# Rotated token inputs formed 1024 columns at a time, attention masks added behind the scores, constants loaded first, and a new table of leads

## Chip, core and metric

The program runs on one core of a Trainium2 chip. The time is the device time of one execution in microseconds (us); lower is better. Inputs lie in the chip's memory in a layout that the host prepares once and that is not timed.

## What is computed

The reference chains three blocks over 2 batches of 768 tokens, everything in float32:

```python
# 1. attention, 8 heads of 64: a window of 31 keys around each query, and the maximum of each block of 32 keys
scores_l = where(|s - t| < 16, scale * q @ k.T, -1e9)
scores_s = scale * q @ max_over_blocks(k) + log(32)
a = softmax(concat(scores_l, scores_s));  x = a @ concat(v, mean_over_blocks(v))
# 2. token mixing by rotation
theta = x @ w_theta
y = w_tok_r @ (x * cos(theta)) + w_tok_i @ (x * sin(theta))
u = x + y;  x2 = u + relu(u @ w_ch)
# 3. gated unit
h = gelu(x2 @ w_in);  u, v = halves(h)
v_s = w_sg @ (layernorm(v) * g) + b_sg
out = x2 + (u * v_s) @ w_out
```

## The kernel before

The eight (batch, two heads) pairs of the attention are worked one after another, each in two halves of 384 queries. For one half, TensorE (PE) forms the scores `S` of two heads, VectorE (DVE) takes the row maxima `nb` (L723), ScalarE (ACT) the exponentials `P` (L728), PE turns `P` round (`PT`, L737), ACT or DVE copies it out (`Pt`), PE multiplies with the values (`O`, L756), DVE divides (`x`, L783), and PE turns the result (`X`, L795) into `xT`. Before that, keys and sums of keys are laid into windows (`kv<-k`, `kv<-ks`) and sums of values (`vsp`, L659) are spread into the value tiles (`kv<-vs`), by whichever of ACT, DVE and GpSimd (POOL) the planner picks.

The 32 score tiles begin with a mask: `masks` multiplies a table of 0 and -8e9 by a bf16 identity with `start=True`, and `mm` adds the products of queries and keys to it (L702, L712).

Every float32 product behind the attention is done as three matmuls of split operands (`mm3`, L443 to L445): high times high, high times low, low times high. `hi_of` makes the high part (ACT, DVE or POOL, L431 to L438), `lo_of` subtracts it for the low part (DVE or POOL, L461). Weights come as raw bits and are put together by a rebias (L552 on ACT, L554 on POOL), three steps on DVE (L541 to L547), and a high and a low part.

The input of the token mixing is split into `xs` (one per 128 tokens, 12 in all), multiplied by `w_th` to angles `th`, reduced to within pi (`rr`), and turned by `rotated(n)`: `abs`, `cos` and `sin` on ACT, then for each of cosine (`cc`) and sine (`rr`) a product with `x` (L876), a high and a low part (`zs`), each over 512 columns. `y_big` and `y_small` multiply them with `w_r`, `w_i` and `w_ri`. From there on (`u`, `ch`, `v`, `sg`, `o`) nothing is edited.

The order of the work is not written out. All operations are declared with a cost per engine, a planner (`Plan`) gives each a due time from the order in which PE work is declared, less a lead by kind (`BIAS`), and plays them out: each engine takes the ready operation that is due first, an operation with a choice of engines goes where cost times a load factor (`LOAD`) is least, and buffers come from pools of a fixed count (`HOMES`). What comes out is one fixed order per engine. SyncE (SP) issues the loads in the order of `PLAN["want"]`; a load that finds no free buffer holds all loads behind it. Each load also waits for the one eight places before it to land.

Where the played-out PE has a gap of over 0.25 us before the operation `warm_end`, filler matmuls are put in (`fill`, L1128, result `wps`, unused); twelve more on zeros open the program (`warm`).

Of the kernel before, what the change touches and what calls it, by code (L numbers as in the profile page):

```python
# [49 lines left out]
class Plan:  # L50
# [266 lines left out]
    "M": 25, "PT": -2, "S": -1, "abs": 4, "ba_": -5, "blocks": 25, "bs_": 8, "bsg": -24,  # L317
    "ch___": -2, "cos": 19, "craw": -6, "g": -5, "gf__": -8, "gm__": -5, "gs__h": -1,
    "gs__l": 15, "id": -18, "ident": 4, "k": 1, "ki": 7, "kk": 13, "kw_": -19, "mask": -10,
    "max": 1, "norm_": 1, "o___": -7, "ob__": 12, "q": -14, "q_": -2, "quarter": -9, "ra": 4,  # L320
    "rb": -4, "rc": -11, "rec_": -3, "sg___": -14, "sin": -6, "small": -4, "sq": 2,
    "st__": 26, "th_": -9, "uT__": 13, "u___": -7, "us__h": 2, "us__l": 8, "v_": -17,
    "v__": 7, "vf_": -4, "vnh_": -4, "vnl_": 21, "vs_": 16, "vsc": -7, "vsg": 1, "vsp": 2,
    "w_ch.": 1, "w_ch.h": -9, "w_ch.hi": -7, "w_ch.lo": 13, "w_i.": -3, "w_i.h": 8,
    "w_i.hi": -12, "w_i.lo": 7, "w_inu.": -9, "w_inu.h": 10, "w_inu.hi": 4, "w_inu.lo": 13,
    "w_inv.": -4, "w_inv.h": 1, "w_inv.hi": 4, "w_inv.lo": -10, "w_out.": 6, "w_out.h": 11,
    "w_out.hi": -14, "w_out.lo": -2, "w_r.": -18, "w_r.hi": -1, "w_r.lo": 9, "w_ri.": 5,
    "w_ri.h": -1, "w_ri.hi": 1, "w_ri.lo": -6, "w_sg.": 8, "w_sg.hi": 24, "w_sg.lo": -7,
# [7 lines left out]
LOAD = ({"ACT": 0.71, "DVE": 1.34, "POOL": 0.92}, {"ACT": 0.08, "DVE": 1.79, "POOL": 23.66},  # L336
        80.0)
# [17 lines left out]
def kernel(  # L355
# [497 lines left out]
    def rotated(n):  # L853

        b, i = divmod(n, NT)
        rr, cc = f"rr{n}", buf(f"cc{n}", "t")
        hf, t = divmod(i, 3)
        x = f"x{b}_{hf}"

        def away(e):  # L860
            if e is ACT:
                e.activation(T(cc)[:], T(rr)[:], AF.Abs)
            else:
                e.tensor_scalar(out=T(cc)[:], in0=T(rr)[:], scalar1=0.0, scalar2=None,
                                op0=ALU.abs_max)
# [2 lines left out]
        op(f"cos{n}", {"ACT": 0.73}, lambda e: ACT.activation(
            T(cc)[:], T(cc)[:], AF.Sin, bias=half_pi[:], scale=-1.0), [cc, "consts"], [cc],
           table="trig", after=last_exp)  # L870
        op(f"sin{n}", {"ACT": 0.62}, lambda e: ACT.activation(T(rr)[:], T(rr)[:], AF.Sin),
           [rr], [rr], table="trig", after=last_exp)
        for k, z in enumerate((cc, rr)):
            zs = f"zs{n}_{k}"
            pair(zs)
            op(f"z{n}_{k}", {"DVE": 0.69, "POOL": 1.28}, lambda e, z=z: e.tensor_tensor(  # L876
                out=T(z)[:], in0=T(z)[:], in1=T(x)[:, t * DM:(t + 1) * DM], op=ALU.mult),
               [z, *((x, r) for r in range(NP))], [z], port=True)
# [4 lines left out]

    def y_big(n):

        b, i = divmod(n, NT)
        for d in range(4):
# [3 lines left out]
            for k, key in enumerate(("r", "i")):  # L891
                op(f"y{n}_{d}_{k}", {"PE": 0.685}, lambda e, d=d, k=k, key=key, y=y: mm3(
                    T(y)[:], cut(hl_of(f"zs{n}_{k}"), sl(d)), unit((key, i)),
                    i == 0 and k == 0, i == NT - 1 and k == 1),
                   [*both(f"zs{n}_{k}"), *has((key, i))], [y])

    def y_small(n):

        b, i = divmod(n, NT)
        for d in range(4):  # L900
# [4 lines left out]
            def mm(e, d=d, y=y):  # L905
                for k in range(2):
                    mm3(T(y)[:, sl(d % 2, 256)], cut(hl_of(f"zs{n}_{k}"), sl(d)),
# [451 lines left out]
```

## Time and profile before

| | us |
|---|---|
| median of 3 runs | 403.67 |
| lowest and highest run | 397.71, 406.56 |
| the profiled execution, device time | 399.96 |
| its span, first to last instruction | 398.2 |
| PE busy within the span | 388.1 |
| DVE, ACT, POOL busy | 282.5, 199.6, 49.0 |

The profile records one execution. A row of `lines` gives a source line, the engine, what is written from what, shape and count, then busy time and mean ns of one instruction, then the idle time before it. A matmul's duration holds its way through the array, so back to back ones overlap: a step from one to the next is shorter than the mean. A row of `windows` gives the busy time of each engine within a stretch, the number of instructions, the granted PE clock, the share of time in which the DMA engines were busy (somewhat over 1 where records overlap) and GB/s. In `waits`, a row says who waited for whom, for how long in total, how often, and the longest.

### The profile page before, as it was taken

The page shows a single profiled execution, that of the slowest core. Times are in us where ns is not written, and L with a number is a line of the kernel's source. Part 1 is how long each engine was busy: PE and PEld are TensorE (multiplying, and loading weights), DVE is VectorE, ACT ScalarE, POOL GpSimd, SP SyncE. Part 2 cuts the span into 40 slices and gives each one's busy share as a digit, 9 for nine tenths or more (in the row PEclk, how much of TensorE's full clock was granted, in tenths as well). Part 3 has the DMA queues.
Part 4 walks back from the last instruction along what each step waited for, and adds up shares of the span by engine and source line. Part 5 has one row for each costly group of instructions (what it writes and reads, how often), then busy time and mean ns, then how long its engine had stood idle before and what let it go on. Part 6 is the DMA issues. An engine that isn't in the chain of part 4 may idle for free.

```text
span 398.2 us, 7273 instructions
## 1 busy us (share of the span) xinstructions
PE 388.1 (97%) x2899; PEld 324.9 (82%) x2899; DVE 282.5 (71%) x542; ACT 199.6 (50%) x415; POOL 49.0 (12%) x81
## 2 busy tenths in 40 slices
PE   7898999999999999999999999999999999999996
PEld 3666667778888888889999988889888889888986
DVE  3769979999999997689999889483454146315442
ACT  3686878668999943244673516274110035411100
POOL 1567886220000000000000000000000000000000
PEclk9999999999999999999999999999999999999999
DMA  8999995310010011338930032010001101000012
GB/s 229 291 282 297 287 252 200 109 54 2 0 34 20 0 54 53 93 96 299 404 130 0 2 106 105 2 53 2 0 0 43 38 28 40 15 0 0 16 44 102
DMA packets 15970, 37.63 MB, mean 95 GB/s; under 512 B 1984, under 2 KB 4928, under 8 KB 15936
## 3 DMA queue, kind: packets, MB, share of 16 engines
q1 hardware_dynamic: 15936, 37.16, 30.0%
q8 instruction: 23, 0.38, 0.4%
q14 instruction: 11, 0.09, 0.1%
HBM read 34.01 MB, written 3.15 MB: 93 GB/s over the span
## 4 chain that ended last, share of the span: by engine, by line
PE 86%; DMA 9%; DVE 3%; SPq 1%; ACT 1%; issue 0%; DVEq 0%
PE y L444 8%; PE y L443 8%; PE y L445 8%; DMA k<-in_kT_dram 4%; PE sg L445 4%; PE sg L444 4%; PE sg L443 4%; PE th L443 3%; PE ch L445 3%; PE ch L443 3%; PE o L445 3%; PE ch L444 3%; PE o L444 3%; PE o L443 3%; PE u L445 3%; PE u L444 3%
## 5 line engine op out<-in xcount | busy, mean ns | idle before, releaser
L431 ACT ACTIVATE g<-gf 128x512 fp32r<-128x512 f32 (+1 forms) x16 | 8.4, 525 | 59.7 <-DVE gf L1100 59.7
L1097 DVE SCALAR_TENSOR_TENSOR gf<-sg,g_sb,bsg 128x512 f32<-128x512 f32 (+1 forms) x16 | 9.9, 617 | 36.4 <-PE sg L445 36.4
L728 ACT ACTIVATE P<-S,nb 128x120 f32<-128x120 f32 x96 | 27.5, 370 | 8.5 <-DVE nb L723 8.1
L444 PE MATMUL y<-w_ri,zs 128*128 128x256 f32 x96 | 27.1, 282 | 0.0
L443 PE MATMUL y<-w_ri,zs 128*128 128x256 f32 x96 | 27.1, 282 | 0.0
L445 PE MATMUL y<-w_ri,zs 128*128 128x256 f32 x96 | 27.0, 282 | 0.0
L443 PE MATMUL ch<-u,w_ch 128*128 128x512 f32 (+1 forms) x64 | 21.7, 338 | 0.0
L445 PE MATMUL ch<-u,w_ch 128*128 128x512 f32 (+1 forms) x64 | 21.6, 338 | 0.0
L444 PE MATMUL o<-g,w_out 128*128 128x512 f32 (+1 forms) x64 | 21.6, 337 | 0.0
L445 PE MATMUL o<-g,w_out 128*128 128x512 f32 (+1 forms) x64 | 21.6, 337 | 0.0
L444 PE MATMUL ch<-u,w_ch 128*128 128x512 f32 (+1 forms) x64 | 21.6, 337 | 0.0
L443 PE MATMUL o<-g,w_out 128*128 128x512 f32 (+1 forms) x64 | 21.6, 337 | 0.0
L444 PE MATMUL u<-x,w_inu 128*128 128x512 f32 (+1 forms) x64 | 21.5, 336 | 0.0
L443 PE MATMUL u<-x,w_inu 128*128 128x512 f32 (+1 forms) x64 | 21.5, 336 | 0.0
L445 PE MATMUL u<-x,w_inu 128*128 128x512 f32 (+1 forms) x64 | 21.5, 336 | 0.0
L443 PE MATMUL th<-w_th,xs 128*128 128x512 f32 x48 | 20.3, 424 | 0.0
L445 PE MATMUL sg<-w_sg,vn 128*128 128x512 f32 x48 | 19.0, 397 | 0.0
L444 PE MATMUL sg<-w_sg,vn 128*128 128x512 f32 x48 | 19.0, 395 | 0.0
L443 PE MATMUL sg<-w_sg,vn 128*128 128x512 f32 x48 | 18.9, 393 | 0.0
L444 PE MATMUL y<-w_i,zs 128*128 128x512 f32 x48 | 18.8, 392 | 0.0
L445 PE MATMUL th<-w_th,xs 128*128 128x512 f32 x48 | 18.8, 392 | 0.0
L444 PE MATMUL y<-w_r,zs 128*128 128x512 f32 x48 | 18.8, 392 | 0.0
(197 smaller groups left out, 1167.3 us busy)
## 6 DMA issues: line engine op xcount, KB each, us to landing
k<-in_kT_dram SPq DMA_DIRECT2D x8, 384.0 KB, 8.1
w_r<-in_w_rT_dram SPq DMA_DIRECT2D x6, 512.0 KB, 6.4
w_i<-in_w_iT_dram SPq DMA_DIRECT2D x6, 512.0 KB, 4.6
kv<-in_vW_dram SPq DMA_DIRECT2D x8, 341.2 KB, 9.3
kv<-in_qT_dram SPq DMA_DIRECT2D x7, 384.0 KB, 9.5
w_th<-in_w_theta_dram SPq DMA_DIRECT2D x4, 512.0 KB, 7.9
w_ch<-in_w_ch_dram SPq DMA_DIRECT2D x4, 512.0 KB, 4.7
w_inv<-in_w_in_dram SPq DMA_DIRECT2D x4, 512.0 KB, 6.2
```

The lines of the kernel that those rows point to most:

```text
L431: e.activation(dst, src, AF.Copy, scale=scale)
L443: PE.matmul(ps, ah, bh, start=first, stop=False, skip_group_check=True)
L444: PE.matmul(ps, ah, bl, start=False, stop=False, skip_group_check=True)
L445: PE.matmul(ps, al, bh, start=False, stop=last, skip_group_check=True)
L728: ACT.activation(T(pt)[:, t * WC:(t + 1) * WC], T(ps)[:, t * WC:(t + 1) * WC], AF.Exp, bias=T(nb)[:, t:t + 1], scale=1.0),
L1097: lambda e: DVE.scalar_tensor_tensor(out=T(gf)[:, :n], in0=T(ps)[:, :n], scalar=g_sb[:, f:f + 1], in1=T("bsg")[:, o:o + n], op0=ALU.mult, ...
```

## The change

`rotated` writes cosine and sine side by side into one tile `zz` of 1024 columns: one product with `x` (read twice, by a repeated axis), one high and one low part, instead of two of each; the halves are cut out in `turned_of`. `scores` sets the matmuls of queries and keys first and the masks behind them, and the masks cover only the 96 window columns of each 120 (288 instead of 360). The constants (`craw`: identity and masks) are the second load instead of the third, and a load of one number out of `craw` (`gate`) stands behind the first queries, so that SP goes on to the values only when `craw` has landed. The opening filler is nine matmuls instead of twelve. All leads, load factors, the place of the third and fourth part of `w_th` among the loads, and of `r 1` and `i 1`, are set anew. Of the tables one line each:

```diff
-HOMES = {"w": 31, "t": 7, "c": 3, ...
+HOMES = {"w": 31, "t": 8, "c": 2, ...
-LOAD = ({"ACT": 0.71, "DVE": 1.34, "POOL": 0.92}, {"ACT": 0.08, "DVE": 1.79, "POOL": 23.66}, 80.0)
+LOAD = ({"ACT": 0.85, "DVE": 0.68, "POOL": 1.1}, {"ACT": 0.05, "DVE": 2.51, "POOL": 23.66}, 70.0)
-    "theta": [20, 26, 27, 28, 29, 36],
+    "theta": [20, 21, 26, 29, 31, 32],
...
         else:
-            load("q0_0", lambda: T("kv0_0")[:, :S // 2], qT[b, r][:, :S // 2], [("q", p, 0)])
             buf("craw", "t")
             load("craw", lambda: T("craw")[:, :P + 3 * WC], consts, ["craw"])
-            load("q0_1", lambda: T("kv0_0")[:, S // 2:S], qT[b, r][:, S // 2:], [("q", p, 1)])
+            for x in range(2):
+                c0 = x * S // 2
+                load(f"q0_{x}", lambda c0=c0: T("kv0_0")[:, c0:c0 + S // 2],
+                     qT[b, r][:, c0:c0 + S // 2], [("q", p, x)])
+
+            op("gate", {"SP": 0.06}, lambda e: e.dma_start(gate[:], T("craw")[0:1, 0:1]),
+               ["craw"], ["gate"], dma=0.01)
...
-        def masks(e):
-            for g in gs:
-                PE.matmul(T(f"S{g}")[:, :3 * WC], id16[:], mask[:, hf * WC:(hf + 3) * WC], start=True,
-                          stop=False, skip_group_check=True)
...
-                                  start=False, stop=True, skip_group_check=True)
+                                  start=t == 0, stop=False, skip_group_check=True)
+
+        def masks(e):
+            def keys(x):
+                return x.rearrange("p (t c) -> p t c", c=WC)[:, :, :WK]
+
+            for g in gs:
+                PE.matmul(keys(T(f"S{g}")[:, :3 * WC]), id16[:],
+                          keys(mask[:, hf * WC:(hf + 3) * WC]), start=False, stop=True,
+                          skip_group_check=True)
...
-        for k, z in enumerate((cc, rr)):
-            zs = f"zs{n}_{k}"
-            pair(zs)
-            op(f"z{n}_{k}", {"DVE": 0.69, "POOL": 1.28}, lambda e, z=z: e.tensor_tensor(
-                out=T(z)[:], in0=T(z)[:], in1=T(x)[:, t * DM:(t + 1) * DM], op=ALU.mult),
-               [z, *((x, r) for r in range(NP))], [z], port=True)
...
+        def turn(e):
+            z = T(zz)[:].rearrange("p (k d) -> p k d", k=2)
+            e.tensor_tensor(out=z, in0=z, in1=T(x)[:, t * DM:(t + 1) * DM].unsqueeze(1)
+                            .to_broadcast([P, 2, DM]), op=ALU.mult)
+
+        op(f"z{n}", {"DVE": 1.22, "POOL": 2.4}, turn,
+           [(zz, 0), (zz, 1), *((x, r) for r in range(NP))], [zz], port=True)
...
+        hi_of(f"zh{n}", hi, lambda: T(zz)[:], [zz], [f"zs{n}_h"], 1024)
+        lo_of(f"zl{n}", lo, lambda: T(zz)[:], hi, [zz, f"zs{n}_h"], [f"zs{n}_l"], 1024)
...
-    op("warm", {"PE": 4.5}, lambda e: fill(12, T("zeros")[:].bitcast(BF16)), ["zeros"], ["wps"])
+    op("warm", {"PE": 3.6}, lambda e: fill(9, T("zeros")[:].bitcast(BF16)), ["zeros"], ["wps"])
```

The order on SP at the start of the program, before (`k0` and `kv0_0<-in_qT` are keys and queries of the first pair, `vW` its values, the name ahead of the arrow is the tile that is written):

```order
L472 DMA k0_79<-in_kT_dram 128x768
L472 DMA kv0_0_81<-in_qT_dram 128x384
L472 DMA craw_83<-in_consts_dram 128x488
L472 DMA kv0_0_81<-in_qT_dram 128x384
L472 DMA kv0_2_86<-in_vW_dram 96x520
L472 DMA kv0_3_90<-in_vW_dram 96x910
L472 DMA kv0_0_81<-in_vW_dram 96x130
L472 DMA k1_93<-in_kT_dram 128x768
```

and now:

```order
L472 DMA k0_80<-in_kT_dram 128x768
L472 DMA craw_82<-in_consts_dram 128x488
L472 DMA kv0_0_84<-in_qT_dram 128x384 x2
L501 DMA gate_72<-craw_82 1x1
L472 DMA kv0_2_104<-in_vW_dram 96x520
L472 DMA kv0_3_110<-in_vW_dram 96x910
L472 DMA kv0_0_84<-in_vW_dram 96x130
L472 DMA k1_114<-in_kT_dram 128x768
```

`craw` moved ahead of the first queries, and the values and all later loads stand behind a load that waits for `craw`.

On PE the program opened with twelve fillers, four masks and then the scores of the first pair; S0 to S3 are its four score tiles, `id16` the bf16 identity:

```order
L1128 MATMUL wps_102<-zeros_88 128x480
L702 LDWEIGHTS id16_67
L702 MATMUL S0_173<-mask_68,id16_67 128x360
...
L702 MATMUL S3_179<-mask_68,id16_67 128x360
L712 MATMUL S0_173<-kv0_1_156,kv0_0_81 64x120
L712 MATMUL S1_175<-kv0_1_156,kv0_0_81 64x120
...
L659 MATMUL vsp0_207<-kv0_2_86,blocks_69 24x130 x2
```

and now it opens with:

```order
L1147 MATMUL wps_89<-zeros_87 128x480
L713 MATMUL S0_133<-kv0_1_101,kv0_0_84 64x120
L713 MATMUL S1_135<-kv0_1_101,kv0_0_84 64x120
...
L722 LDWEIGHTS id16_67
L722 MATMUL S0_133<-mask_68,id16_67 128x3x96
...
L722 MATMUL S3_180<-mask_68,id16_67 128x3x96
L1147 LDWEIGHTS id16_67
L1147 MATMUL wps_89<-mask_68,id16_67 128x480
...
L664 MATMUL vsp0_218<-kv0_2_104,blocks_69 24x130 x2
```

The scores come first, the masks and four new fillers stand between them and the sums of values. In all there are 18 fillers on the mask instead of 9, and 9 on zeros instead of 12.

On POOL, where the first angles are prepared (`xs0<-xT` with one source is the high part of 128 tokens' input, with two sources its low part; `w_r` and `w_i` with one source are rebiases, which need the weight's load), it stood before:

```order
L554 TENSOR_SCALAR w_i0_374<-w_i0_374 128x512
L433 TENSOR_SCALAR xs0_887<-xT_75 128x512
L433 TENSOR_SCALAR kv4_2_141<-vs_71 24x520
L461 TENSOR_TENSOR xs0_887<-xT_75,xs0_887 128x512
L461 TENSOR_TENSOR w_th2_928<-cw_th2_815,w_th2_928 128x512
L433 TENSOR_SCALAR xs1_971<-xT_75 128x512
```

and now:

```order
L461 TENSOR_TENSOR w_th2_936<-cw_th2_739,w_th2_936 128x512
L433 TENSOR_SCALAR xs1_1026<-xT_76 128x512
L433 TENSOR_SCALAR xs2_1041<-xT_76 128x512
L559 TENSOR_SCALAR w_r1_731<-w_r1_731 128x512
L559 TENSOR_SCALAR w_i1_737<-w_i1_737 128x512
L461 TENSOR_TENSOR xs1_1026<-xT_76,xs1_1026 128x512
L461 TENSOR_TENSOR xs2_1041<-xT_76,xs2_1041 128x512
```

The rebiases of `w_r1` and `w_i1`, which ACT did before (L552), now stand on POOL between the high and the low part of `xs1`. PE's first angles are now those of `xs1` (before: `xs0`), and ahead of them PE has the whole fifth pair, counted from zero, instead of its first half.

## Rows read from the trace of the kernel before

**Rows 1.** Busy time of each engine in stretches (us from the span's start)

```profile
14.70:53.40 38.70, 34.47 (x607) 25.24 (x607) 31.22 (x69) 29.56 (x85) 27.41 (x45) 1.00 1.05 286
...
60.00:100.00 40.00, 40.00 (x464) 31.32 (x457) 37.88 (x78) 30.79 (x72) 10.84 (x13) 1.00 0.27 89
...
340.00:380.00 40.00, 40.00 (x222) 34.63 (x221) 13.90 (x23) 7.77 (x15) 0.00 (x0) 1.00 0.03 11
```

**Rows 2.** Who waited for whom: PE's waits

```profile
PE X L795 <- DVE x L783: 3.8, 5, 0.9
```

**Rows 3.** PE in order of time, the opening: start us, us, what, count

```profile
1.49 4.98 PE L1128 MATMUL wps<-zeros 128*128 128x480 bf16 x12 [1.49 <-DVE zeros L1137]
7.19 0.77 PE L702 MATMUL S<-mask,id 128*128 128x360 bf16 x4 [0.72 <-DVE mask L438]
7.89 1.46 PE L712 MATMUL S<-kv,kv 64*64 64x120 f32 x48
9.28 2.96 PE L659 MATMUL vsp<-kv,blocks 96*24 96x130 f32 x24
```

**Rows 4.** Groups of PE instructions by line

```profile
L702 PE MATMUL S<-mask,id 128*128 128x360 bf16 x32 | 7.4, 318 | 0.7 <-DVE mask L438 0.7
...
L1128 PE MATMUL wps<-mask,id 128*128 128x480 bf16 x9 | 3.0, 370 | 0.0
```

**Rows 5.** SP in order of time, the first loads

```profile
0.74 0.38 SPq L472 DMA_DIRECT2D k<-in_kT_dram  x1
...
1.64 0.42 SPq L472 DMA_DIRECT2D craw<-in_consts_dram  x1
...
2.58 1.37 SPq L472 DMA_DIRECT2D kv<-in_vW_dram  x3
```

**Rows 6.** Everything on the tile craw: us from issue to landing

```profile
DMA to landing us min/median/max: 4.9/4.9/4.9
```

**Rows 7.** DVE in order of time: the first work on landed keys, the first maxima

```profile
3.71 0.95 DVE L614 TENSOR_REDUCE ks<-k 128x24 f32<-128x768 f32 x1 [2.27 <-DMA k<-in_kT_dram]
...
8.79 1.85 DVE L723 TENSOR_REDUCE nb<-S 128x3 f32<-128x360 f32 x4 [0.96 <-PE S L712]
```

**Rows 8.** Groups of DVE instructions by form

```profile
L876 DVE TENSOR_TENSOR cc<-cc,x 128x512 f32<-128x512 f32 x12 | 8.2, 686 | 0.0
L1100 DVE TENSOR_TENSOR gf<-gf,uT 128x512 f32<-128x512 f32 x8 | 5.5, 692 | 0.3
L1100 DVE TENSOR_TENSOR gf<-gf,uT 128x256 f32<-128x256 f32 x8 | 3.4, 425 | 0.3
L438 DVE COPY Pt<-PT 120x384 f32<-120x384 f32 x3 | 1.6, 549 | 0.2 <-PE PT L737 0.2
L438 DVE COPY kv<-vs 24x910 f32<-24x910 f32 x2 | 2.2, 1094 | 0.1
```

**Rows 9.** PE in order of time: scores of two halves running, the first angles

```profile
46.96 0.85 PE L712 MATMUL S<-kv,kv 64*64 64x120 f32 x24
...
51.13 1.06 PE L712 MATMUL S<-kv,kv 64*64 64x120 f32 x24
...
53.87 0.48 PE L443 MATMUL th<-w_th,xs 128*128 128x512 f32 x1
```

**Rows 10.** SP in order of time, around the first angles

```profile
50.11 1.38 SPq L472 DMA_DIRECT2D w_r<-in_w_rT_dram  x2
57.82 0.33 SPq L472 DMA_DIRECT2D w_i<-in_w_iT_dram  x1
```

**Rows 11.** DMA issues from 46 to 56 us: count, KB each, median us to landing

```profile
w_i<-in_w_iT_dram SPq DMA_DIRECT2D x1, 512.0 KB, 8.6
```

**Rows 12.** POOL, DVE and PE in order of time, first angles and first y

```profile
58.86 1.28 POOL L461 TENSOR_TENSOR xs<-xT,xs 128x512 fp32r<-128x512 f32 x1
...
99.09 0.68 DVE L461 TENSOR_TENSOR zs<-cc,zs 128x512 fp32r<-128x512 f32 x1
...
101.88 0.39 PE L443 MATMUL y<-w_r,zs 128*128 128x512 f32 x1
```

More of the change, by code (lines that the diff above doesn't have):

```diff
@@ L316 @@
 BIAS = {
[L317 to L328, printed above, removed]
@@ L329 @@
-    "w_sgs.": 1, "w_sgs.hi": -8, "w_sgs.lo": 8, "w_th.": 1, "w_th.h": -4, "w_th.lo": -2,
-    "warm": -21, "warm_end": -10, "xT_": -5, "x__": 8, "xh": 2, "xs__h": 3, "xs__l": -13,
-    "y__": 2, "ys_": -14, "z_": 2, "zeros": -13, "zh_": -6, "zl_": -2,
+    "M": 25, "S": -1, "abs": 4, "ba_": -5, "blocks": 25, "bs_": 16, "bsg": -24, "ch___": -6,
+    "cos": 18, "craw": -6, "g": -9, "gf__": -12, "gm__": -5, "gs__h": -6, "id": -22,
+    "ident": 8, "k": 5, "ki": 7, "kk": 13, "ksum": 1, "kw_": -19, "mask": -12, "max": 1,
@@ new lines @@
+    "norm_": 2, "o___": -3, "ob__": 12, "q": -4, "q_": -2, "quarter": -13, "rb": -8, "rc": -9,
+    "rec_": -3, "sg___": -14, "sin": -6, "small": -6, "sq": 2, "th_": -9, "uT__": 13,
+    "u__": -6, "u___": -7, "us__h": -6, "us__l": 8, "v_": -13, "v__": 3, "vf_": -8,
+    "vnh_": -4, "vnl_": 21, "vs_": 14, "vsc": -7, "vsg": 1, "vsp": -6, "vsw_": 4, "w_ch.": 1,
+    "w_ch.h": -9, "w_ch.hi": -7, "w_ch.lo": 13, "w_i.": -3, "w_i.h": 9, "w_i.hi": -12,
+    "w_i.lo": 7, "w_inu.": -17, "w_inu.h": 10, "w_inu.hi": -4, "w_inu.lo": 5, "w_inv.": -2,
@@ new lines @@
+    "w_inv.h": 1, "w_inv.hi": 4, "w_inv.lo": -10, "w_out.": 6, "w_out.h": 11, "w_out.hi": -14,
+    "w_out.lo": 2, "w_r.": -14, "w_r.hi": -1, "w_r.lo": 9, "w_ri.": 4, "w_ri.h": -1,
+    "w_ri.hi": 1, "w_ri.lo": -7, "w_sg.": 8, "w_sg.hi": 24, "w_sg.lo": -7, "w_sgs.": 1,
+    "w_sgs.hi": -7, "w_sgs.lo": 8, "w_th.": 1, "w_th.h": -3, "w_th.lo": -2, "warm": -21,
+    "warm_end": -14, "xT_": -5, "x__": 9, "xh": -2, "xs__h": 7, "xs__l": -13, "y__": 2,
+    "ys_": -14, "z_": 2, "zeros": -13, "zh": 2, "zh_": -6, "zl_": -2,
@@ L334 @@
 STAY = 15.5
-LOAD = ({"ACT": 0.71, "DVE": 1.34, "POOL": 0.92}, {"ACT": 0.08, "DVE": 1.79, "POOL": 23.66},
-        80.0)
+LOAD = ({"ACT": 0.85, "DVE": 0.68, "POOL": 1.1}, {"ACT": 0.05, "DVE": 2.51, "POOL": 23.66},
+        70.0)
 PLAN = {
-    "want": [("pair", 0), ("pair", 1), ("th", 0), ("pair", 2), ("pair", 3), ("th", 1), ("pair", 4),
-             ("th", 3), ("th", 2), ("pair", 5), ("r", 0), ("i", 0), ("pair", 7), ("pair", 6),
-             ("i", 1), ("r", 1)],
+    "want": [("pair", 0), ("pair", 1), ("th", 0), ("pair", 2), ("pair", 3), ("th", 1), ("pair", 4), ("th", 2), ("pair", 5), ("th", 3), ("r", 0), ("i", 0), ("pair", 7), ("pair", 6),
+             ("r", 1), ("i", 1)],
     "ahead": 0,
-    "theta": [20, 26, 27, 28, 29, 36],
+    "theta": [20, 21, 26, 29, 31, 32],
     "filler": 20,
@@ L417 @@
     vs_sb = cp.tile([P, VC], F32, tag="vs", name="vs")
+    gate = cp.tile([1, 1], F32, tag="gate", name="gate")
     half_pi = cp.tile([P, 1], F32, tag="hpi", name="half_pi")
@@ L855, in rotated @@
         b, i = divmod(n, NT)
-        rr, cc = f"rr{n}", buf(f"cc{n}", "t")
+        rr, zz = f"rr{n}", buf(f"zz{n}", "w")
         hf, t = divmod(i, 3)
         x = f"x{b}_{hf}"
+        for k in range(2):
+            plan.at((zz, k), zz)
         def away(e):
             if e is ACT:
-                e.activation(T(cc)[:], T(rr)[:], AF.Abs)
+                e.activation(T(zz)[:, 512:], T(rr)[:], AF.Abs)
             else:
-                e.tensor_scalar(out=T(cc)[:], in0=T(rr)[:], scalar1=0.0, scalar2=None,
+                e.tensor_scalar(out=T(zz)[:, 512:], in0=T(rr)[:], scalar1=0.0, scalar2=None,
@@ L865, in away @@
                                 op0=ALU.abs_max)
-        op(f"abs{n}", {"ACT": 0.62}, away, [rr], [cc], port=True)
+        op(f"abs{n}", {"ACT": 0.62}, away, [rr], [(zz, 1)], port=True)
         op(f"cos{n}", {"ACT": 0.73}, lambda e: ACT.activation(
[L869 to L872, printed above, removed]
@@ new lines, in rotated @@
+           [(zz, 1), "consts"], [(zz, 1)], table="trig", after=last_exp)
+        op(f"sin{n}", {"ACT": 0.62}, lambda e: ACT.activation(T(zz)[:, :512], T(rr)[:], AF.Sin),
+           [rr], [(zz, 0)], table="trig", after=last_exp)
+        def turn(e):
[4 more added lines that the diff above has]
+           [(zz, 0), (zz, 1), *((x, r) for r in range(NP))], [zz], port=True)
@@ L892, in y_big @@
                 op(f"y{n}_{d}_{k}", {"PE": 0.685}, lambda e, d=d, k=k, key=key, y=y: mm3(
[L893 removed]
+                    T(y)[:], cut(turned_of(n, k), sl(d)), unit((key, i)),
                     i == 0 and k == 0, i == NT - 1 and k == 1),
[L895 removed]
+                   [f"zs{n}_h", f"zs{n}_l", *has((key, i))], [y])
     def y_small(n):
@@ L911, in y_small @@
             op(f"ys{n}_{d}", {"PE": 0.73}, mm,
-               both(f"zs{n}_0") + both(f"zs{n}_1") + has(("ri", i)), [y])
+               [f"zs{n}_h", f"zs{n}_l", *has(("ri", i))], [y])
     def x_keys(b, half, d):
```

16 lines of the change are left out of this document (9 added, 7 removed).

## The prediction

> **What bounds the kernel now.** I read the windows first. From 60 us PE is busy without a gap: of eight stretches of 40 us up to 380 us each shows 40.00 us of PE, the first and the last stand in [rows 1]. DVE, ACT and POOL have time left in them. So work taken off DVE, ACT or POOL behind 60 us is worth nothing, and the end can move only through PE's own work, and through gaps ahead of 60 us. In the attention, from 14.7 to 53.4 us, no engine is full [rows 1]: of 38.7 us PE has 34.47, DVE 31.22, ACT 29.56 and POOL 27.41, and only the DMA share (1.05, at 286 GB/s) is at its limit. The waits name one steady wait of PE there: `X` waits for `x` on DVE, 3.8 us in five waits [rows 2]. In order of time the opening comes next [rows 3]: twelve fillers, masks, scores, then `vsp`, which ends at 12.24 us because it waits for the values.
>
> **The sum's base.** Durations come from one execution of 399.96 us, its span 398.2 and 1.76 around it. That is 3.7 below the median of three runs (403.67), inside their 397.71 to 406.56. I sum against 399.96. A measurement of this kernel can tell about 2%, 8.1 us, from no change.
>
> **The change part by part.**
>
> Narrow masks. Each of 32 masks loses 72 of its 360 columns. The price of a column comes from two groups [rows 4]: 480 columns take 370 ns, 360 take 318, so 52 ns for 120 columns, 31 ns for 72; 32 of them give 1.0. PE has gaps around them, so some of it may be hidden; and the read now jumps from block to block, which no row shows. Bounded by a full gain and by the 52 ns as a loss each (32 x 0.052): -1.0 to +1.7. I take -1.0, since the number of columns is what the rows price.
>
> Scores ahead of masks. The first scores stand behind the masks, which wait for a DVE copy of `craw` and start at 7.19 [rows 3]; `craw` is issued at 1.64 [rows 5] and lands 4.9 us later [rows 6]. Now the scores need only keys and queries, `craw` is issued one load (0.4 to 0.5 us) earlier and should land at about 5.2, and the masks end at about 8.2, where the first row maxima could start on scores at 8.79 [rows 7]. Gain 0.6. Bounds: -1.5 if `craw` lands so early that the masks never wait, +0.5 if it lands at 6.5 as before and the masks' 0.77 us then stand behind the scores. I take -0.6.
>
> The gate. SP issues the values at 2.58 [rows 5]; now SP waits for `craw` and goes on at about 5.3. `k` (384 KB), `craw` (244) and `q` (384) are 1.01 MB ahead of it, at 286 GB/s [rows 1] 3.5 us, done at about 6.0 with the start. `k`, issued at 0.74, lands at 3.71 [rows 5, 7], 2.97 us, of which 384 KB at 286 GB/s are 1.35; so 1.6 us of a load is no transfer, and the values' first bytes come at about 7.0. That is a hole of 1.0 us in a stream that is full from the first loads on through the attention [rows 1]. Queued behind the gate on SP is every later load. I take +0.9; bounds 0 (the stream has the slack) and +2.7 (5.3 less 2.58, all of it passed on).
>
> For the part of a load that is no transfer the Trainium skill ("DMA: Bandwidth & Descriptors", section "Anatomy of one DMA — SWDGE (gpsimd) path") states about 2 us, most of it the confirmation that the last byte has landed. By it the hole would be 1.4 us and the term +1.3; the trace's 1.6 us is used. The rule speaks against this edit: a load that waits for another's landing pays that time once more.
>
> Fillers. Three fewer on zeros are 3 x 0.415 [rows 3] off a stretch that ends before the scores can start: worth nothing, covered by the wait for `k` and `q`. Nine more on the mask cost by the price of a column above 480 x 0.43 ns = 0.21 us each, 1.9 in all. Four stand ahead of `vsp`, which waited for values until 12 us in any case; the planner puts the others where it sees gaps. I take +0.5; bounds 0 and +1.9.
>
> Where the helpers of the attention run. By the order, up to the maxima of the twentieth score tile DVE gets seven more copies of `PT` (7 x 0.549 = 3.8 by [rows 8]) and two wide copies of sums of values (2 x 1.094 = 2.2, [rows 8]), 6.0 us, and smaller pieces leave it, on an engine that has 7.5 us free of 38.7 [rows 1], while ACT and POOL get lighter. Against that `X` now stands further behind `O` on PE, so that its waits of 3.8 us [rows 2] could go. What is late next, if they go, is DVE itself with its maxima. I take +0.5; bounds -3.8 (all waits go) and +6.0 (all of DVE's added work reaches the end); the value near nothing, since both ends draw on the same free 7.5 us.
>
> First angles. Ahead of the first `th` at 53.87 PE now has half a pair more, 4.2 us from one half's scores to the next (46.96, 51.13) [rows 9], and six new fillers beside the four counted, 1.3; so it gets there at about 59.4. There it needs the low part of `xs1`, which POOL now does behind the rebiases of `w_r1` and `w_i1`. Two such loads were issued at 50.11, the second ends its issue at 51.49 [rows 10], and one takes 8.6 us to land [rows 11], so between 58.5 and 60.1; I take the early end, since the order wants them sooner. A rebias (an estimate: half of the low part's, with one source for two, 0.64) and the low part (1.28, [rows 12]) give 60.5: PE waits 1.1, with a share of the gate's shift 1.4. Queued behind that `xs1` on POOL is the low part of `xs2`, and on PE the angles of both. Bounds: 0 (the weights land by 57.5) and +8.9 (below).
>
> The rotation. Two products of 686 ns [rows 8] become one of 1024 columns. From 256 to 512 columns a like product goes from 425 to 692 ns [rows 8], 267 for 256; so 692 + 534 = 1.23 us against 1.37, for 24 products and low parts -3.5 us on DVE, and less on ACT too. All of it lies beside a full PE [rows 1]: worth nothing. If the cover is gone, it is at the first `y`: it needs a cosine's low part alone, done at 99.77, 2.1 us ahead of `y` at 101.88 [rows 12]; now it waits for both halves, which costs from 0 to +1.2. I take 0.
>
> Sum: -1.0 - 0.6 + 0.9 + 0.5 + 0.5 + 1.4 + 0 = +1.7, so 399.96 + 1.7 = 401.7.
>
> **The rivals.**
>
> Late weights under POOL (slower). Place: the rebias of `w_i1` ahead of the low part of `xs1`. SP issued two `w_r` at 50.11, but a `w_i` only at 57.82 [rows 10], when a buffer came free. If the first `w_i` needed gets such a late place, it lands at 57.82 + 8.6 = 66.4 [rows 11], the low part ends at 68.3, and PE stands for 8.9 us; at 59.5 the wait is 2.1. The mean is 5.5 in place of 1.4: 405.8. It decides as soon as `w_i1` lands behind 57.5. For it: the queue's rows, and no other work of PE between. Against: the planner sees loads and buffers and placed POOL's row there; PE may also be later than 59.4.
>
> Waits of the attention gone (faster). The 3.8 us of `X` [rows 2] vanish since `X` has more work ahead of it, and the weights land in time: 399.96 - 1.0 - 0.6 + 0.9 + 0.5 - 3.8 = 396.0. For it: the new order sets just these apart, and ACT (29.56 of 38.7) and POOL lose work. Against: DVE, which ends the wait, gets more.
>
> The clock of the opening (slower by a little). The twelve fillers step at 415 ns for 480 columns [rows 3], 1.16 columns to the ns, the level of 1.2 GHz; the four masks behind them go 1440 columns in 0.77 us, above it. With nine fillers PE has been busy for 1.25 us less when the scores start. If these run at the lower level, their 1.46 and the masks' 0.65 double: +2.1, 403.8. Against: the fillers end before the scores in either case and could be enough.
>
> The Trainium skill ("TensorE: Matmul & The Clock Gate", section "Part 1: The HAM clock gate") has the low clock as the resting state, which activity releases; the fillers' step and the masks' agree with it.
>
> That the change doesn't do what it says holds for the rotation: it does save DVE's time, but PE doesn't wait for it.
>
> **How the numbers follow.** Forecast 401.7 (with its own spread of 3 either side) .50; late weights .18; attention waits gone .24; clock .06; something else .02. The range that holds 8 in 10 reaches from the faster rival (396.0, less 1 for the sizes of its terms) to the slower one with its larger waits (399.96 + 0.3 + 8.9 = 409.2): 395 to 409; the forecast's own is 398.7 to 404.7. Faster by over 2% is below 395.6 (of the median): nearly half of the faster rival and a little of the forecast, .16. Slower by over 2% is above 411.7: the late weights at their worst with the gate's 2.7 or the attention's 6.0 on top, .10. The rest, .74, is within 2%.
>
> **What would show it.** In the profile after: first scores at about 6 us, ahead of `craw`'s landing at about 5.2 plus a copy; masks of a mean near 288 ns; a DMA share well under 0.9 in a stretch between 5 and 8 us (the hole); one wait of PE `th` for POOL `xs`, 1 to 2 us long; products of 1024 columns on DVE at about 1.23 us; PE 40.00 of 40 from 60 on. Wrong would make it: a wait of `th` over 4 us (the weights), `X` without waits and DVE not full (the faster rival), first scores of twice 1.46 us (the clock), or a gap of PE behind 60 us that before didn't have, at the first `y` above all.

## The result, and the profile after

The changed kernel takes 405.48 us (median of 20 runs, 401.32 to 407.85), the kernel before 402.73 (20 runs): ratio 1.0111, 95% interval 1.0084 to 1.0137, some 4.5 us slower (1.11% of 402.73). The ratios in this document leave out runs over 1.5% above the fastest of the same kernel, here 7 of 20 before and 2 of 20 after; over all runs the medians differ by 2.75 us, and the means give ratios lower by 0.1 to 0.7 points for every kernel but `e12`. The profiled execution took 403.10 us, its span is 401.3.

The opening first. SP's loads and PE in order of time, changed kernel:

```profile
1.18 0.42 SPq L472 DMA_DIRECT2D craw<-in_consts_dram  x1
...
4.51 0.71 SPq L501 DMA_DIRECT2D gate<-craw  x1
5.27 1.29 SPq L472 DMA_DIRECT2D kv<-in_vW_dram  x3
```

```profile
1.50 3.78 PE L1147 MATMUL wps<-zeros 128*128 128x480 bf16 x9 [1.50 <-DVE zeros L1156]
5.21 2.48 PE L713 MATMUL S<-kv,kv 64*64 64x120 f32 x48
7.62 0.66 PE L722 MATMUL S<-mask,id 128*128 128x288 bf16 x4
8.12 0.97 PE L1147 MATMUL wps<-mask,id 128*128 128x480 bf16 x4
9.02 2.84 PE L664 MATMUL vsp<-kv,blocks 96*24 96x130 f32 x24
```

Against [rows 3, 5]: the values are issued at 5.27 instead of 2.58, the scores start at 5.21 instead of 7.89, but take 2.48 us instead of 1.46. Windows of the changed kernel (columns as in [rows 1]: the last two are DMA share and GB/s):

```profile
4.00:5.00 1.00, 1.00 (x4) 0.17 (x2) 1.00 (x3) 1.00 (x4) 0.69 (x3) 1.00 0.92 343
5.00:6.00 1.00, 1.00 (x17) 0.80 (x20) 0.89 (x6) 0.30 (x2) 0.47 (x2) 1.00 0.01 5
6.00:7.00 1.00, 1.00 (x28) 1.00 (x24) 0.04 (x1) 0.00 (x0) 0.00 (x0) 1.00 0.67 149
...
14.70:53.40 38.70, 33.49 (x596) 24.10 (x592) 31.24 (x70) 25.83 (x82) 18.31 (x35) 1.00 1.04 292
60.00:100.00 40.00, 40.00 (x473) 31.77 (x472) 36.89 (x74) 34.10 (x84) 6.76 (x7) 1.00 0.21 68
```

The stream stands still from 5 to 6 us (5 GB/s) and is half empty to 7. Behind 60 us PE is full as before; the loss lies ahead of it. PE's waits:

```profile
PE X L805 <- DVE ri L796: 3.1, 1, 3.1
PE O L766 <- POOL kv L433: 2.0, 1, 2.0
...
PE O L766 <- DVE Pt L438: 1.0, 2, 0.7
...
PE X L805 <- DVE x L793: 0.3, 1, 0.3
```

The five waits of [rows 2], 3.8 us, are down to one of 0.3; two new ones, 5.1 us, have come. Where they lie, PE and then DVE in order of time:

```profile
46.52 0.97 PE L1147 MATMUL wps<-mask,id 128*128 128x480 bf16 x4
49.46 0.94 PE L766 MATMUL O<-kv,Pt 120*64 120x65 f32 x24 [1.97 <-POOL kv L433]
50.33 0.85 PE L713 MATMUL S<-kv,kv 64*64 64x120 f32 x24
51.11 0.42 PE L722 MATMUL S<-mask,id 128*128 128x288 bf16 x2
51.37 0.37 PE L1147 MATMUL wps<-mask,id 128*128 128x480 bf16 x1
54.82 0.59 PE L805 MATMUL X<-ident,x 128*128 128x128 f32 x3 [3.09 <-DVE ri L796]
55.21 0.85 PE L747 MATMUL PT<-ident,P 128*120 128x128 f32 x3
55.99 1.53 PE L664 MATMUL vsp<-kv,blocks 96*32 96x130 f32 x24
...
61.55 0.48 PE L443 MATMUL th<-w_th,xs 128*128 128x512 f32 x1
```

```profile
48.96 0.54 DVE L438 COPY kv<-vs 24x130 f32<-24x130 f32 x1
51.92 0.95 DVE L619 TENSOR_REDUCE ks<-k 128x24 f32<-128x768 f32 x1 [2.43 <-DMA k<-in_kT_dram]
52.79 0.15 DVE L796 TENSOR_SCALAR ri<-O 128x6 f32<-128x6 f32 x1
52.91 1.07 DVE L436 TENSOR_SCALAR kv<-ks 128x192 f32<-128x192 f32 x1
53.91 0.18 DVE L799 RECIPROCAL ri<-ri 128x6 f32<-128x6 f32 x1
54.12 0.56 DVE L793 TENSOR_TENSOR x<-O,ri 128x384 f32<-128x384 f32 x1
```

DVE stands at the sums of the last keys (`ks<-k`) from 49.5 until they land, at 51.92. The division `ri`, whose `O` is old, stands behind it, `X` behind that, and PE runs dry. On POOL it is the same with the keys before:

```profile
45.92 0.99 POOL L433 TENSOR_SCALAR kv<-k 128x672 f32<-128x672 f32 x2 [1.75 <-DMA k<-in_kT_dram]
46.87 0.78 POOL L433 TENSOR_SCALAR kv<-ks 128x192 f32<-128x192 f32 x1
47.62 0.61 POOL L433 TENSOR_SCALAR w_th<-cw_th 128x512 fp32r<-128x512 f32 x1
48.32 1.09 POOL L433 TENSOR_SCALAR kv<-vs 24x520 f32<-24x520 f32 x1
```

The last line is what `O` at 49.46 waits for. After the gap PE is slow for a while: `vsp` takes 1.53 us where it took 0.87; the window from 55 to 60 us has a granted clock of 0.66, between the levels of 1.2 and 2.4 GHz:

```profile
55.00:60.00 5.00, 5.00 (x66) 3.74 (x64) 3.35 (x6) 2.33 (x9) 3.69 (x6) 0.66 0.52 179
```

In the kernel before the last keys are started on at 51.66, no earlier, and DVE's order there is of the same kind (DVE, then PE):

```profile
51.66 0.95 DVE L614 TENSOR_REDUCE ks<-k 128x24 f32<-128x768 f32 x1 [1.42 <-DMA k<-in_kT_dram]
52.53 0.15 DVE L786 TENSOR_SCALAR ri<-O 128x6 f32<-128x6 f32 x1
...
52.95 0.56 DVE L783 TENSOR_TENSOR x<-O,ri 128x384 f32<-128x384 f32 x1
```

```profile
53.56 0.55 PE L795 MATMUL X<-ident,x 128*128 128x128 f32 x3 [0.91 <-DVE x L783]
```

But `X` starts 1.90 us behind the start on the keys there and 2.90 us now, since the copy `kv<-ks` (1.07 us) now stands between `ri` and its reciprocal. And PE's first `th` ran from 53.87 on [rows 9], ahead of the rest of the attention; now it runs at 61.55.

### The profile page after: what moved, and what is told of

It reads as the page before. It is cut to its first block, busy times and chain, and to the rows that moved or that the text cites. A ratio compares the mean times of both kernels' runs of the same rounds, so it can differ in the third digit from the quotient of the medians.

```text
span 401.3 us, 7245 instructions
## 1 busy us (share of the span) xinstructions
PE 389.7 (97%) x2905; PEld 326.5 (81%) x2905; DVE 286.1 (71%) x526; ACT 198.7 (50%) x415; POOL 33.3 (8%) x61
## 4 chain that ended last, share of the span: by engine, by line
PE 88%; DMA 9%; DVE 1%; SPq 1%; issue 0%
PE y L445 8%; PE y L444 8%; PE y L443 8%; DMA k<-in_kT_dram 5%; PE sg L443 4%; PE sg L444 4%; PE sg L445 4%; PE th L443 3%; PE o L444 3%; PE u L443 3%; PE o L443 3%; PE u L445 3%; PE ch L445 3%; PE u L444 3%; PE o L445 3%; PE ch L444 3%
## 5 line engine op out<-in xcount | busy, mean ns | idle before, releaser
L431 ACT ACTIVATE g<-gf 128x512 fp32r<-128x512 f32 (+1 forms) x16 | 8.4, 524 | 64.1 <-DVE gf L1119 58.7
L444 PE MATMUL y<-w_ri,zs_h 128*128 128x256 f32 x96 | 27.0, 282 | 0.0
L443 PE MATMUL y<-w_ri,zs_h 128*128 128x256 f32 x96 | 27.0, 282 | 0.0
L445 PE MATMUL y<-w_ri,zs_l 128*128 128x256 f32 x96 | 27.0, 282 | 0.0
L443 PE MATMUL th<-w_th,xs 128*128 128x512 f32 x48 | 20.1, 418 | 0.0
L444 PE MATMUL v<-w_inv,x 128*128 128x512 f32 x48 | 18.9, 394 | 0.0
L443 PE MATMUL v<-w_inv,x 128*128 128x512 f32 x48 | 18.9, 394 | 0.0
L445 PE MATMUL y<-w_i,zs_l 128*128 128x512 f32 x48 | 18.9, 394 | 0.0
```

The costliest lines, as they stand in the source:

```text
L431: e.activation(dst, src, AF.Copy, scale=scale)
L443: PE.matmul(ps, ah, bh, start=first, stop=False, skip_group_check=True)
L444: PE.matmul(ps, ah, bl, start=False, stop=False, skip_group_check=True)
L445: PE.matmul(ps, al, bh, start=False, stop=last, skip_group_check=True)
```

## The experiments

Each profile gives the time at which DVE starts on the last keys and the span. A summary, worked out from the profiles (`e11` is left out: its profiled execution took 406.14 us, 2.4 more than its median). "Last keys" is DVE's start on the keys that land last; in `e2`, `e3` and `e10` DVE comes to them without a wait, so they had landed by then:

```
kernel                  gate  last keys  span   span less keys  ratio to before [95%]
before                  no    51.66      398.2  346.5           1
e9_before_gate          yes   56.11      402.6  346.5           1.0101 [1.0019, 1.0183]
changed                 yes   51.92      401.3  349.4           1.0111 [1.0084, 1.0137]
e14_after_again         yes   50.17      398.0  347.8           1.0043 [0.9990, 1.0097]
e2_sums_late            yes   50.83      398.6  347.8           1.0022 [0.9970, 1.0075]
e4_twelve               yes   53.89      403.2  349.3           1.0082 [1.0013, 1.0151]
e3_fill_gap             yes   53.55      405.5  352.0           1.0120 [1.0044, 1.0196]
e1_no_gate              no    47.92      395.8  347.9           1.0026 [0.9975, 1.0078]
e10_no_gate_late        no    50.05      398.0  348.0           1.0054 [1.0004, 1.0105]
e5_before_tables        yes   52.35      403.0  350.7           1.0179 [1.0105, 1.0252]
f3_old_tables_no_gate   no    52.12      402.2  350.1           1.0086 [1.0035, 1.0138]
e6_after_tables         no    53.36      401.6  348.2           1.0130 [1.0037, 1.0223]
e13_before_whole        no    53.73      402.7  349.0           1.0086 [1.0043, 1.0130]
e12_before_keys_first   no    47.84      399.3  351.5           0.9999 [0.9955, 1.0043]
f1_rate_no_gate         no    52.64      400.6  348.0           1.0011 [0.9963, 1.0059]
f4_rate_gate            yes   53.75      400.3  346.6           1.0063 [1.0014, 1.0113]
f2_before_rate          no    56.61      400.9  344.3           0.9998 [0.9946, 1.0050]
```

The last column but one belongs to one order of the work (346.5 twice, 347.8 and 347.9 in `e14` and `e1`) and doesn't compare orders: `f2` has the least, 344.3, and no better time. That the loads wait for PE, rather than PE for the loads, would be another reading. The traces speak against it: of SP's waits from 8 to 44 us, when the last keys have been issued in both, 19.9 of 20.9 us in the changed kernel and 22.7 of 23.1 in the kernel before are for earlier loads to land.

**The gate taken out, and put into the kernel before.** `e1_no_gate` replaces `lambda e: e.dma_start(gate[:], ...)` by `lambda e: None`; nothing else moves.

> The changed kernel without the load of one number that SP waits for; every other instruction stands where it stood. Theory 'queues' (PE's new waits come from the landing of the last keys and from ready work that stands behind them in the queues of DVE, POOL and ACT): the hole of about 1 us in the DMA stream goes, the last keys land about 1 us earlier than 51.9, the waits of 2.0 and 3.1 us stay in place, and the time falls by 0 to 1.3 us. Rival 'stream' (the gate's delay of all later loads is what the change costs): the time falls by 3 to 4.5 us, back to the kernel before.

Ratio 1.0026: 0.85 points (+- 0.6) or 3.4 us less than the changed kernel, what the rival 'stream' expected. The profile has the last keys at 47.92, 4 us earlier; the waits stay but shrink (`X` 1.5, `O` 0.4). Its window where the hole was:

```profile
5.00:6.00 1.00, 0.85 (x24) 0.65 (x24) 0.83 (x6) 0.21 (x2) 0.38 (x2) 1.00 1.10 356
...
0.00:14.00 14.00, 11.41 (x128) 7.14 (x130) 8.00 (x21) 7.73 (x22) 2.89 (x14) 1.00 0.89 274
```

The changed kernel, with the gate, in the same window:

```profile
0.00:14.00 14.00, 12.29 (x121) 7.87 (x121) 7.74 (x20) 7.55 (x22) 2.90 (x14) 1.00 0.77 235
```

274 less 235 GB/s over 14 us are 0.55 MB, 1.8 us at 300 GB/s. `e9_before_gate` adds the gate to the kernel before, behind `q0_1`:

```diff
         o.fn(ENG[o.on])
+        if o.name == "q0_1":
+            SP.dma_start(gate[:], T("craw")[0:1, 0:1])
```

> The kernel before with one thing added: SP's load of one number out of the constants behind the first queries, as in the changed kernel; no other instruction moves. Theory 'gate': all later loads move back by the hole, 1 to 2 us, the last keys land at 52.7 to 53.7 us instead of 51.7, and the ratio is 1.003 to 1.008. If the stream has slack: ratio 0.998 to 1.002.

Ratio 1.0101, just above what was expected; the last keys come 4.45 us later and the span is 4.4 longer, so that what lies behind them is 346.5 in both. Its window, and under it that of the kernel before:

```profile
0.00:14.00 14.00, 10.66 (x96) 6.30 (x96) 6.39 (x17) 6.13 (x18) 3.57 (x16) 1.00 0.71 214
```

```profile
0.00:14.00 14.00, 11.79 (x120) 6.91 (x120) 7.15 (x18) 7.07 (x21) 4.12 (x16) 1.00 0.89 242
```

28 GB/s over 14 us, 0.39 MB, 1.3 us. The rest of the 4.45 us is no part of the hole: the landing scatters in one and the same kernel too, as the next run shows.

**The changed kernel once more.** `e14_after_again`, unaltered.

> The changed kernel once more, unaltered. Theory 'landing' (in one kernel the span is the time at which DVE starts on the last keys plus a constant; the kernel before and the kernel before with the gate both gave 346.5 us, the changed kernel 401.3 - 51.92 = 349.4): wherever the last keys land in this execution, the span is 348.4 to 350.4 us behind it. Rival: the span varies for other reasons, and the difference falls outside these bounds as soon as the landing differs by over 1 us.

The keys landed 1.75 us earlier, and the span fell by 3.3: 347.8 behind the keys, outside what was expected. The missing 1.6 us is the clock: `X` waits 0.8 us instead of 3.1, and PE does not slow down. `X` starts 2.9 us behind the start on the keys in both, but from there to the first `th` this run takes 5.17 us and the changed kernel's first profile 6.73 (54.82 to 61.55):

```profile
53.08 0.52 PE L805 MATMUL X<-ident,x 128*128 128x128 f32 x3 [0.85 <-DVE ri L796]
...
58.25 0.47 PE L443 MATMUL th<-w_th,xs 128*128 128x512 f32 x1
```

```profile
55.00:60.00 5.00, 5.00 (x89) 4.02 (x91) 4.65 (x10) 4.96 (x16) 3.97 (x5) 1.00 0.64 226
```

So by these profiles the changed order costs 347.8 less 346.5, 1.3 us, at an equal landing (1.0 of it on the way from the keys to `X`, shown above), and 1.6 more where the keys come so late that the clock falls. `e4_twelve`, at 349.3, agrees (granted clock 0.91 from 44 to 62 us, as in the changed kernel). The ratio of this run is 1.0043 [0.9990, 1.0097]: one and the same kernel measured twice differs by 0.68 +- 0.6 points, as much as most of the edits here move it. Both together give 1.0098.

**Ready work put ahead of the late keys.** `e2_sums_late` moves three operations after planning; `e10_no_gate_late` does so without the gate.

```diff
     done = plan.run()
+    at = {o.name: o for o in done}
+    late = [at[x] for x in ("ksum6", "ksw6_0", "ksw6_1")]
+    done = [o for o in done if o not in late]
+    i = done.index(at["norm4_0"]) + 1
+    done[i:i] = late
```

> The changed kernel with the reduction of the last keys (ks<-k, and the two copies of its result) moved on DVE and ACT behind the two divisions x that stood behind it; nothing else moves. Theory 'queues': the wait of 3.1 us of X goes to under 0.5, the clock stays at its upper level between 52 and 60 us, which gives back another 1 us or so, and the time falls by 2.5 to 4 us. Rival 'stream': PE waits as long at its next instruction that needs the last keys, and the time falls by less than 0.7 us. Rival 'clock': nothing but the clock decides, gain 1.3 us.

> The changed kernel with both: no gate, and the reduction of the last keys behind the divisions. If the two losses add up: ratio to the kernel before 0.992 to 0.996, faster than both kernels. If they are one and the same loss (the wait for the last keys): 1.000 to 1.003, as either alone.

PE and DVE of `e2_sums_late` in order of time:

```profile
51.05 0.49 PE L805 MATMUL X<-ident,x 128*128 128x128 f32 x3
...
59.27 0.50 PE L445 MATMUL th<-w_th,xs 128*128 128x512 f32 x1 [1.58 <-POOL xs L461]
```

```profile
49.00 0.16 DVE L796 TENSOR_SCALAR ri<-O 128x6 f32<-128x6 f32 x1
...
50.83 0.94 DVE L619 TENSOR_REDUCE ks<-k 128x24 f32<-128x768 f32 x1
```

`X` no longer waits, and the ratio falls to 1.0022, 0.9 points less (3.6 us, inside what was expected). But 347.8 us lie behind the keys, as in `e14`: the wait went on to `th`, 1.6 us for POOL's `xs`. What the move saves in the profiles is the clock's loss, 1.6 us; the keys also come 1.1 us earlier here, as they may in any run. Against both measurements of the changed kernel the gain is 0.8 +- 0.6 points. With both edits the ratio is 1.0054 [1.0004, 1.0105], a little above what was expected of a single loss and no better than either edit alone: the two losses don't add up, which fits one loss, the wait for the last keys.

**Fillers.** `e3_fill_gap` puts 9 fillers ahead of that `O` and 14 ahead of that `X`; `e4_twelve` restores `fill(12, ...)` at the start.

> The changed kernel with 9 and 14 more filler matmuls on PE ahead of the O that waits 2.0 us and the X that waits 3.1 us, so that PE is busy there but does nothing more. Theory 'clock' (a part of the loss is the lower clock behind the gap): vsp, X and PT at 55 to 59 us take 0.87, 0.5 and 0.5 us again instead of 1.53, 0.9 and 0.69, and the time falls by about 1.3 us. If the clock's dip is without effect: 0. 'Queues' and 'stream' expect the two waits to be filled, and no more than the clock's 1.3 us.

> The changed kernel with 12 fillers on zeros at the start instead of 9. Theory 'clock': the first scores, which took 2.48 us behind nine fillers, take about 1.46 us again but start 1.25 us later: +0.2 us at the row maxima, and 0 to +0.3 us in the time. If the scores are slow for another reason: they stay at 2.48 us and everything in the opening is 1.25 us later.

`e3`: 1.0120, no gain. `vsp` takes 0.87 us again behind the gap, but the clock had fallen earlier (0.80 from 40 to 50 us), PE came to the place late, and the fillers were in its way; it decides nothing about the clock. `e4`: the first scores start 1.2 us later, at 6.41, and take 1.70 us. With nine fillers they took 2.48, 2.35, 2.00 and 1.46 us in four runs of the same opening (changed, `e14`, `e3`, `e2`). The granted clock reads 1.00 in all windows of the opening, so which level PE is on can be told only from steps: the nine fillers on zeros take 0.42 us each, the four on the mask behind the scores 0.24, for 480 columns both. By them the rise falls now ahead of the scores, now into them, and as all four durations occur with nine fillers, their number alone does not decide. Neither edit is worth anything measurable.

**Code and tables apart.** `e5_before_tables`: the changed code under the old `HOMES`, `BIAS`, `LOAD` and `PLAN`; `f3_old_tables_no_gate`: the same without the gate; `e6_after_tables`: the old code under the new tables; `e13_before_whole`: the old kernel with only `rotated` and `turned_of` exchanged.

> The changed kernel's code (rotation over 1024 columns, narrow masks behind the scores, constants first, gate, nine fillers) under the old tables of leads, load factors, buffers and load order. Theory 'gate' (the hole behind the gate costs about 3 us whatever the order): ratio to the kernel before 1.006 to 1.010. Theory 'queues' (the new tables put reductions of late keys ahead of ready work and the angles behind the attention): ratio 1.000 to 1.003. If both hold in part: about 1.005.

> The changed code under the old tables (as e5_before_tables, ratio 1.018) without the gate. Theory 'gate': 2 to 3.5 us less than with it, ratio 1.008 to 1.012. Rival: the loss of that mixture lies in its order alone, ratio 1.014 or above.

> The kernel before in its code (rotation by halves, full masks ahead of the scores, no gate, twelve fillers) under the new tables. Theory 'gate': ratio 0.998 to 1.002, since there is no gate. Theory 'queues': ratio 1.006 to 1.011, with waits of PE for DVE and POOL of over 3 us together between 44 and 58 us.

> The kernel before with the rotation alone formed over 1024 columns, under the old tables, planned anew. My prediction's step: worth nothing, ratio 0.997 to 1.003, since PE is full from 60 us on. Rival: the coarser grain or the buffers of the new tile cost PE a wait behind 60 us, ratio 1.005 or above.

1.0179, 1.0086, 1.0130 and 1.0086. Each of these parts, planned anew, is slower than the kernel before, and without the gate the whole (`e1`, 1.0026) isn't measurably so: the parts don't add up. `e5` and `e6` lie above all that was expected, and `e6` doesn't have the waits that 'queues' put there: of 18 us from 44 to 62 PE is busy 17.18 (before: 17.09). What the new tables alone cost stays open. Without the gate the mixture loses 0.9 points of its 1.8, as `e1` did. In `e13` the order is that of the kernel before up to the keys of the last two pairs and another from there: PE waits 1.3 us for the exponentials at 54.97 and 0.7 for `x` at 66.76, and is full behind 70. That the order costs, and not the rotation, is argued from this: no run has the rotation in an unchanged order. The narrow masks, the masks behind the scores and the early `craw` have no run of their own either.

**Loads.** `e11_keys_first_ng` (without the gate) and `e12_before_keys_first` put the last two pairs ahead of the first `r` and `i` (and of `th 3`) in `want`.

> The changed kernel without the gate and with the last part of w_th and the first w_r and w_i (1.5 MB) behind the last two pairs among the loads; the order is planned anew. Theory 'landing': the last keys land some 5 us earlier than 47.9 to 50.1 (the two runs without the gate), at 43 to 45 us, and the span falls until PE itself is the bound: ratio to the kernel before 0.982 to 0.993. Rival 'angles': the weights behind the keys are then late for the first angles and for y, PE waits there instead, and the ratio is 1.000 or above.

> The kernel before with the first w_r and w_i (1 MB) behind the last two pairs among the loads; the order is planned anew. Theory 'landing': the last keys land 3 to 3.5 us earlier than 51.7, and the ratio is 0.990 to 0.995. Rival 'angles': 1.000 or above, with waits of PE for POOL or DVE at th or y.

1.0033 [0.9994, 1.0071] and 0.9999 [0.9955, 1.0043]: no gain. In `e12` the last keys do land earlier, by 3.8 us, about as 'landing' has it (DVE, then PE):

```profile
47.84 0.95 DVE L614 TENSOR_REDUCE ks<-k 128x24 f32<-128x768 f32 x1 [2.32 <-DMA k<-in_kT_dram]
```

```profile
50.27 0.55 PE L795 MATMUL X<-ident,x 128*128 128x128 f32 x3 [2.37 <-DVE x L783]
```

But the planner moved their sums forward with them, to 44.26 us by its own time. DVE again stands 2.3 us for the keys, PE 2.4 for the `x` behind them, and 351.5 us lie behind the keys, 5.0 more than in the kernel before. So the theory's step that failed is that the span follows the landing: it does in one order, not in one that is planned anew for the earlier landing. (In `e11` DVE starts on the last keys at 49.86, not at 43 to 45.)

**Planned with the landing that the traces show.** `f1_rate_no_gate`, `f4_rate_gate` and `f2_before_rate` set `RATE = 275e3` instead of `300e3` in the plan.

> The changed kernel without the gate, planned with 275 instead of 300 GB/s for loads, so that the plan itself has the last keys land at about 52 us, as the traces show, instead of 48. The reductions of keys then stand behind the divisions, and the first angles ahead of the scores of the sixth pair. Theory 'order' (the changed kernel loses because its order trusts a landing that comes 3.7 us later): the span is at most 347 us behind the landing of the last keys, no wait of X over 1.5 us, ratio to the kernel before 0.990 to 1.000. Rival 'stream': ratio as without the gate alone, 1.000 to 1.005.

> The same with the gate. Theory 'gate' (the hole moves the last keys by some 1.5 to 2 us in any order): 1.5 to 3 us slower than f1_rate_no_gate. If the order decides alone: as f1_rate_no_gate within 1 us.

> The kernel before, planned with 275 instead of 300 GB/s. Theory 'order': the kernel before had only a small part of this loss (waits of 0.9 us of X), so the ratio is 0.993 to 1.003. If any new plan of this kernel is slower, as with the rotation alone: 1.005 or above.

1.0011, 1.0063 and 0.9998. `f1` misses two of its bounds (348.0 behind the keys, not 347; ratio above 1.000). No wait of PE for DVE is over 0.6 us, but PE came later to the place and found waits elsewhere (1.7 us of `S` for nothing that the profile shows, 1.2 for queries). `f4` against `f1` is the gate once more, +0.52 points.

**The gate in five orders.** Differences with and without it: 0.85 (changed), 1.01 (before), 0.93 (old tables), 0.52 (planned with 275 GB/s) and -0.32 (sums behind the divisions, `e2` against `e10`), each by itself uncertain by 0.6 to 0.9. Weighted by the intervals the mean is 0.59 +- 0.32 points, 2.4 us, of the 1.11 that the change costs (0.80 +- 0.36 without the last pair). In the same five pairs of profiles DVE starts on the last keys 4.0, 4.45, 0.2, 1.1 and 0.8 us later with the gate. So the gate costs time, but how much is known only roughly, and whether it costs anything where ready work stands ahead of the keys is not shown. For the remaining 0.5 (+- 0.4) the runs show no more than the 1.3 us behind the keys, and the clock's 1.6 where it falls. No version here is measurably faster than the kernel before.

## Why the prediction was wrong

It named 401.7 us, below the median of the kernel before, while its own sum was +1.7. The step that failed first is the sum's base: the sum was put onto one execution of 399.96 us, although the three runs known then had a median of 403.67; the median of 20 runs is 402.73. On that the sum would have given 404.4. The range held 405.48; the direction did not come out, since the base was one of the faster executions of a kernel whose runs spread over 9 us.

That the sum itself comes near is in part luck. In the profiled pair PE stands still for 8.4 us up to 62 us instead of 6.8 (fillers count as work), and 1.6 us go to the lower clock: together the 3.1 us by which the spans differ. The prediction had waits there too, but for other reasons. The steps:

- **Gate** (+0.9, bounds 0 to +2.7): mis-sized, as far as the pairs tell. The place and the start were right (values at 5.27, said 5.3; a hole between 5 and 7 us). The hole was 1.0 to 1.8 us in five pairs of profiles, said 1.0, and the time lost 2.4 +- 1.3. I had taken the hole's own length as the price; what waits for the last keys adds to it, in the changed kernel's first profile the clock's 1.6 us. By the Trainium skill ("DMA: Bandwidth & Descriptors", section "Anatomy of one DMA — SWDGE (gpsimd) path"; about 2 us of a DMA that are no transfer, fitted there to loads that GpSimd issues) the estimate was +1.3: within the hole that the runs show, and at the lower end of what the gate cost.
- **First angles** (+1.4, a wait of `th` for POOL's `xs`): wrong place. The weights came as said (rebias of `w_i` at 58.40; POOL does the low parts of `xs1` and `xs2` from 59.01 to 61.53, so the first is done at about 60.3, said 60.5), but PE was there only at 61.55, because it had stood 5.1 us before that for `O` and `X`. In `e2` and `e10`, where ready work stands ahead of the keys, the wait of `th` is there, 1.6 and 1.5 us; in `e14` and `e1`, where `X` waits 0.8 and 1.5, it isn't. So it is right in kind for another order, and no part of this one. (In the working, 50.11 and 8.6 are 58.7, not 58.5, which changes little.)
- **Helpers of the attention** (+0.5): the waits of `X` for `x` went, 3.8 to 0.3, as the faster rival had it. The step that failed is what is late next: the prediction put DVE there with its maxima, and the runs show DVE and POOL standing for late keys, 5.1 us of PE's waits in the first profile and 0.8 in `e14`. What that rival and the forecast missed is in-order queues: sums of keys stand ahead of ready divisions, and the keys land 3.7 us later than the planner has them (51.92 against its own time of 48.25 for `ksum6`; in the kernel before 51.66 against 47.93). The trace of before showed it, a DVE wait for keys at 51.66, which I had not read.
- **Narrow masks** (-1.0): right, 291 ns instead of 318, 32 x 27 ns = 0.9 of PE's time; what of it reaches the end no run shows.
- **Opening** (-0.6): right; maxima at 7.95 instead of 8.79. `craw` landed at 4.5 (said 5.2), scores at 5.21 (said 6.0). The clock rival's place was right too, with 1.0 of its 1.5 us of scores, in some runs; an effect on the end is not shown.
- **Fillers** (+0.5): not measurable.
- **Rotation** (0): duration right, 1219 ns (said 1.23); behind 70 us PE is full in both kernels. But the zero was said of a fixed order: alone and planned anew it cost 0.86 points, which I had not priced.

Groups of the changed kernel by line and form, from which these durations are:

```profile
L461 DVE TENSOR_TENSOR zs_l<-zz,zs_h 128x1024 fp32r<-128x1024 f32 x12 | 14.6, 1219 | 1.7 <-PE y L445 1.7
L888 DVE TENSOR_TENSOR zz<-zz,x 128x1024 f32<-128x1024 f32 x12 | 14.5, 1219 | 0.0
...
L722 PE MATMUL S<-mask,id 128*128 128x288 bf16 x32 | 6.5, 291 | 0.0
```

## What to carry to other kernels

Where a stage lives from a full DMA stream, look for the instruction in each engine's queue that waits for the last transfer, and for what stands ready behind it: an order that trusts an early landing turns a late one into idle time on the engines behind it (here DVE, POOL and PE), and an earlier load doesn't help when the order is planned for it (`e12`). A wait on the loading engine leaves a hole in the stream, and what depends on the last load can pay for it, so price it at that load and not where it stands. Put a sum of microseconds onto the median of many runs, not onto the one that was profiled, and measure one kernel twice before you explain a difference of half a point.

## What was not expected

The landing of the last keys differs by 1.75 us between two runs of one kernel (51.92 and 50.17), and by 2 more in `e4` with three more fillers (53.89), at a DMA share of 1.04 in all three from 14 to 44 us; most of the spread of 398 to 407 us may come from there, but what sets the stream's rate in an execution stays open. In several runs PE stood still for nothing that the profile shows, up to 2.4 us ahead of an `O` in `e3`; that too stays open.
